# One core, eight batches of attention and a two-layer block: a written order that runs to the end of batch 2 and holds the loads, batch 0's exp sums by adds, 128-column products, half-width output tiles

## The chip, the core and the metric

The kernel runs on one core of a Trainium2 chip. The metric is the time of one execution in device microseconds; lower is better. The core has five engines with a queue each: TensorE (PE, with its weight loads as PEld), VectorE (DVE), ScalarE (ACT), GpSimd (POOL) and SyncE (SP). The kernel is written so that each engine works through its own instructions in the order in which the program names them, and waits where another engine or a transfer isn't done.

## The reference

Inputs are q, k and v of shape (8, 12, 448, 64) and two weight matrices, all float32; the output is (3584, 768) in float32.

```python
scores = q @ k^T / sqrt(64)
e = exp(scores - max)
attn = e / (sum(e) + exp(-max) + 1e-9)
x = (attn @ v), heads side by side        # (8*448, 768)
h = x @ w_in                              # (3584, 2048)
out = relu(h)**2 @ w_out                  # (3584, 768)
```

The kernel computes exp of the scores without the maximum, and 1 / (sum + 1) for the divisor, which is the same; constant scales (`GS`, L43) are taken out in the last copy.

## The kernel before

**Tiling.** A batch is 448 tokens. Its 12 heads are taken in three quads of four heads; the 448 keys of a head in seven chunks of 64. Scores of one chunk and one quad are four products on quarters of the array (64 rows by 64 columns, shape 64*64 in the profile), which run side by side and write one `sp` tile of two banks; one exp on ScalarE turns it into float16. Such a pair is a visit. Sums of exps for later batches come from adds on VectorE (`add_quad`, L384, four steps) and one product with ones for the quad (`sums_of_quad`, L400); then Ln and Exp on ScalarE give the reciprocal (`quad_z`, L412), products with v give the values (`values_step`, L424, seven steps), and VectorE multiplies both into `xt` (`quad_x`, L436). First-layer blocks are 128 of the 2048 hidden columns: six products of 128 rows each, relu (`relu`, L469, on either engine) into `rt`, and a square on VectorE (`squared`, L476) into `gs`. An output half-tile is 128 tokens by 384 columns: 16 products over the hidden blocks (`out_piece`, L553), then a scaled copy (`out_done`, L569) and a store (`store`, L539, in SP's queue).

**Shapes of the products.** `product` (L457) issues one product of 128*128, or, in mode COLS2, two of 128*64. Mode SQUARE, for output tiles among scores (L744), splits each into four products of 64*64. Transposes (L202, L228) are of shape 128*64.

**Batch 0** is done in two halves of 224 queries, so that its first-layer blocks can start early. One piece is `half_scores` (L262), `half_exp` (L283) and `post` (L298), which multiplies the exps with v and with ones for the sum. The sums of a half are so on TensorE: a product for every key chunk. `half_z` (L318) and `half_x` (L324) follow. `xp`, the tile of values and sums, has one buffer.

**The written order.** From the start to the middle of batch 2 the program is a list of steps, `ORDER` (L684): s scores, e exp, p post, z and x the end of a half, T and U a transpose and its copy, a S Z v X the steps of a quad, i r g a first-layer block of a half of batch 0 (a pair of blocks of 224 columns), q R G a pair of blocks of batch 0 by row tiles (`Square`, L505: 64*64 products, with a no-op of SP's queue between the two halves of the contraction), o O an output half-tile, W warm-up products, c t u the first quad's casts, transposes and copies, P the change from two product tiles (beside `xp`) to a ring of four (L678). Products in the list are in mode COLS2 (L682). Steps s0 to s23 and e0 to e23 are batch 0, s24 and later the quads of batches 1 and 2, seven visits each. The list ends with s55, that is four visits into the second quad of batch 2, and after three output half-tiles (`EARLY`, L44).

**Loads** are GpSimd's (DMA with a cast to float16), issued in this order: batch 0's other quads, v of batch 0, w_in in quarters (each in two issues), batch 1's q and k and v, then with step L0 batch 2's first two quads and w_out in quarters, with L1 the rest of batch 2 and the copy of batch 3 into a float16 stage in DRAM. Natural q and k lie in two tiles, `nn0` and `nn1`, one buffer each, so a load into one waits for the transposes that read it.

**Behind the list** runs a loop over b (L770). For b = 2 it does the 16 first-layer blocks of batch 1 in mode COLS2, visits of batch 2 between output half-tiles in mode SQUARE, and values of batch 2's first two quads. From b = 3 on each pass is the same: values and visits among output half-tiles, then eight blocks, visits among output tiles, and eight more blocks; q and k come transposed by DMA in SP's queue (L168), with a copy on GpSimd (L179) and a stage for the batch after the next. The end is products alone, in mode FULL.

Of the kernel before, what the change touches and what calls it, by code (L numbers as in the profile page):

```python
# [16 lines left out]
def kernel(  # L17
# [26 lines left out]
    EARLY = 3  # L44
    IN_HALVES = 8
# [13 lines left out]
    osb_pool = ctx.enter_context(tc.tile_pool(name="osb", bufs=2))  # L59
# [32 lines left out]


    def mm(out_, lhsT, rhs, start, stop):
        return nc.tensor.matmul(out_, lhsT, rhs, start=start, stop=stop)  # L95
# [202 lines left out]
    def post(at):  # L298

        g, half, _ = HALVES[at]  # L300
        if (g, half) not in xzs:
            xzs[g, half] = xp_pair()
        xz, e = xzs[g, half], half_e(g, half)
        two = pieces(at)
        todo = sorted(two[0] + two[1])
        for is_sum in range(2):
            for c, j in todo:
                for i in range(2):
                    r = slice(64 * i, 64 * i + 64)
                    key = (g, half, i, j)  # L310
# [3 lines left out]
                    opened.add(key)  # L314
# [140 lines left out]
    ots = {}  # L455
# [49 lines left out]
    class Square:  # L505


        def __init__(self, t0, f0):
            self.t0, self.f0 = t0, f0
            self.hp, self.done, self.last = None, 0, None  # L510

        def part(self, flip, c0, c1):
            if self.hp is None:
                self.hp = [mp_tile(), mp_tile()]
            hp, xt = self.hp, xts[self.t0 // S]
            assert flip == self.done // DCH
            for dc in range(c0, c1):
                self.done += 1
                for o in range(2):
                    r = (o + flip) % 2  # L520
                    rows_ = slice(64 * r, 64 * r + 64)
                    for y in (0, 64):
                        f = (self.f0 + o) * 128 + y
                        got = mm(hp[o][y:y + 64, 0:S], win[rows_, dc, f:f + 64], xt[rows_, dc, :],
                                 start=self.done == 1, stop=self.done == 2 * DCH)
                        if self.last:
                            after(got, self.last)
                            self.last = None
            if self.done == DCH:
                self.last = nc.sync.nop()  # L530
                after(self.last, got)

        def relu(self, o, act):
            relu(self.hp[o], (self.t0, self.f0 + o), S, act)

        def squared(self, o):
            squared((self.t0, self.f0 + o), self.t0, S, self.f0 + o, 1)

    def store(c, ot, n0, n1):  # L539
        end = c + 128  # L540
        while c < end:
# [6 lines left out]
            nc.sync.dma_start(out=rows[t, p:p + m, :], in_=ot[o:o + m, n0:n1])  # L548
# [65 lines left out]
    nat0 = nat.tile([128, RUN * 2 * S], FP16, name="nn0")  # L614
    load_natural_quads(0, (1, 2), 0, nat0)
    for g in range(NQ):
        load_v_quads(0, g, g + 1)
    NW = 4
    for i in range(NW):
        load_win(i, NW)  # L620
    load_natural_quads(1, (0,), 0, nat.tile([128, RUN * 2 * S], FP16, name="nn1"))
    load_v_quads(1)
    load_natural_quads(1, (1, 2), 0, nat.tile([128, RUN * 2 * S], FP16, name="nn0"))
# [9 lines left out]
    squares = [Square(0, f0) for f0 in range(IN_HALVES, NFFB, 2)]  # L633

    def loads_later():
        load_natural_quads(2, (0, 1), 0, nat.tile([128, RUN * 2 * S], FP16, name="nn1"))
        for n0 in (0, HALF):
            for y in range(2):
                load_wout(n0, y, 2)

    def loads_last():
        load_natural_quads(2, (2,), 0, nat.tile([128, RUN * 2 * S], FP16, name="nn0"))
        load_v_quads(2)
        stage(3)

    def quad_visit(n):
# [17 lines left out]
        "q": lambda n, flip, c0=0, c1=DCH: squares[n].part(flip, c0, c1),  # L664
        "R": lambda n, o, act: squares[n].relu(o, act),
        "G": lambda n, o: squares[n].squared(o),
# [15 lines left out]
    mode[0] = COLS2  # L682

    ORDER = """  # L684
        W9 c0,0,0 c1,0,0 t0,0,0 c1,4,1 c0,4,0 t1,0,0 u0,0,0,0 u1,0,0,0 t1,0,4 t0,0,4 u1,0,4,1 s0 u0,0,4,0 t1,1,0
        u1,1,0,0 t0,1,0 s1 u0,1,0,0 t0,1,4 e0 t1,1,4 u0,1,4,0 e1 u1,1,4,0 s2 T0,1,1 T0,1,0 U0,1,1 s3 T0,2,0 e2
        e3 U0,1,0 s4 T0,2,1 s5 e4 U0,2,0 p0 s6 p1 e5 e6 s7 e7 p2 p3 U0,2,1 s8 z0 s9 e8 x0 e9 p4 s10 p5 s11 e10
        p6 p7 s12 e11 z1 e12 s13 x1 p8 s14 e13 p9 e14 s15 e15 p10 p11 s16 s17 z2 x2 e16 p12 s18 p13 e17 e18 s19
        p14 s20 p15 e19 z3 i0,3 i0,0 x3 r0,3,0 e20 p16 s21 r0,0,1 p17 s22 p18 T1,0,0 g0,3 e21 g0,0 e22 U1,0,0
        p19 s23 T1,0,1 i0,1 U1,0,1 z4 s24 x4 e23 s25 e24 p20 p21 s26 e25 e26 p22 r0,1,0 s27 p23 z5 T1,1,0 g0,1  # L690
        U1,1,0 i0,2 x5 s28 T1,1,1 r0,2,1 i1,1 e28 U1,1,1 L0 g0,2 e27 i1,0 r1,1,1 s29 r1,0,1 g1,1 s30 T1,2,1 a0,0
        g1,0 U1,2,1 e29 i1,2 s31 e30 a0,1 a0,2 r1,2,1 s32 g1,2 P0 T2,1,0 e32 e31 a0,3 i1,3 T1,2,0 L1 s33 U2,1,0
        r1,3,1 U1,2,0 q1,0,0,3 e33 s34 v0,0 g1,3 q1,0,3,6 e34 S0 v0,1 q1,1,0,3 v0,2 s35 v0,3 a1,0 q1,1,3,6 v0,4
        v0,5 R1,0,0 Z0 s36 e35 R1,1,1 v0,6 G1,0 e36 s37 X0 T2,1,1 T2,0,0 e37 s38 T2,0,1 e38 U2,1,1 s39 q0,0,0,3
        G1,1 s40 q0,0,3,6 e39 s41 U2,0,1 e40 U2,0,0 v1,0 q0,1,0,3 s42 a1,1 a1,2 e41 v1,1 a1,3 q0,1,3,6 v1,2 S1
        R0,1,0 e42 v1,3 a2,0 R0,0,1 s43 v1,4 q2,0,0,3 Z1 v1,5 q2,0,3,6 v1,6 X1 s44 e43 G0,1 G0,0 q2,1,0,3 e44
        s45 q2,1,3,6 e45 R2,0,0 q3,0,0,3 R2,1,1 s46 q3,0,3,6 s47 e46 e47 v2,0 q3,1,0,3 s48 v2,1 G2,1 G2,0
        q3,1,3,6 v2,2 e48 s49 a2,1 v2,3 R3,0,0 e49 R3,1,0 s50 G3,1 o1,0,4 a2,2 s51 G3,0 a2,3 v2,4 e50 o1,4,8
        v2,5 e51 s52 a3,0 S2 v2,6 e52 o2,0,4 o1,8,12 o2,4,8 a3,1 o1,12,16 Z2 X2 s53 e53 s54 o2,8,12 o0,0,4 a3,2
        e54 a3,3 T2,2,0 O1 U2,2,0 S3 s55 o0,4,8 T2,2,1 o0,8,12 o2,12,16 U2,2,1 O2 e55 o0,12,16 Z3 O0  # L700
# [28 lines left out]
    del outs[0:EARLY]  # L729

# [39 lines left out]
    for b in range(2, B):  # L770
        m = NQ * (b - 1)
        if b > 2:
            n = min(3, len(outs))
            ns = 12 * PIECE + n * TILE + KC * PIECE
            work = chain(timed(values_quad(m - 1)), second(n))
# [62 lines left out]
```

## Time and profile before

| what | value |
|---|---|
| time, median of 3 runs | 407.54 us (407.45 to 409.01) |
| the profiled execution: its time | 407.19 us |
| the profiled execution: its span, first to last instruction | 405.4 us |
| granted TensorE clock | 1.000 |
| time to landing of a quarter of w_out (768 KB) | 15.6 us |
| DMA, whole span | 45.38 MB, mean 112 GB/s |

Sizes of the loads as the profile lists them: q or k of one quad 224 KB, v of one quad 224 KB, an issue of w_in 384 KB, one of w_out 768 KB, the stage of q or k 676 KB, v of a whole batch 672 KB, and for batch 0's first quad q and k in two parts, 224 KB each in float32 and 112 KB each in float16.

How to read it: a row of the timeline has the start in us, the time, the engine, the line, the operation, out<-in, shapes and the count of merged instructions, and in brackets the idle time before it with what ended it. `64*64`, `128*64` and `128*128` are rows by columns of the array that a product uses. Products overlap in the records (their ends are modelled), so rates are taken from start to start. A row of groups has, behind the bar, the busy time, the mean ns of one instruction and the idle time before it. A row of DMA issues has the count, the KB of each and the median us to landing.

### The profile page before, as it was taken

The numbers are of one execution on the slowest core, as the hardware profiler recorded it, in microseconds if no ns is written. First come the engines' busy times: TensorE is split into PE (matmuls) and PEld (weight loads), VectorE is DVE, ScalarE is ACT, GpSimd is POOL, SyncE is SP. The second block draws the span as 40 slices with busy tenths as digits, with TensorE's granted clock in tenths as the row PEclk, the third lists the DMA queues.
The fourth block names the chain that finished last, engine by engine and source line by source line (L and its number), as shares of the span: only waits on it lengthen the run. The fifth ranks groups of instructions, "written<-read, shape, count | busy, mean of one in ns | idle before, by whom it ended". The sixth has DMA issues, their size and how long they took to land.

```text
span 405.4 us, 14903 instructions
## 1 busy us (share of the span) xinstructions
PE 392.2 (97%) x6861; PEld 260.8 (64%) x6861; DVE 258.9 (64%) x466; ACT 222.0 (55%) x279; POOL 60.1 (15%) x95
## 2 busy tenths in 40 slices
PE   8878999999999999999999999999999999999996
PEld 4656856657676766767676666767566675555654
DVE  3214778776967777686867777686867868186000
ACT  4897899718375565827475564827366473100111
POOL 8444220005000320006000430005000000000000
PEclk9999999999999999999999999999999999999999
DMA  8999999196908693196907593196401020100222
GB/s 147 204 205 204 204 204 212 31 191 123 213 9 128 140 183 85 42 189 112 222 12 150 118 185 83 42 189 104 103 3 40 3 81 2 57 23 0 79 78 78
DMA packets 70846, 45.38 MB, mean 112 GB/s; under 512 B 46720, under 2 KB 65280, under 8 KB 70784
## 3 DMA queue, kind: packets, MB, share of 16 engines
q0 software_dynamic: 24720, 22.62, 35.6%
q1 hardware_dynamic: 45776, 21.59, 23.5%
q8 instruction: 53, 0.87, 0.9%
q10 hardware_dynamic: 288, 0.23, 0.2%
q14 instruction: 9, 0.07, 0.1%
HBM read 45.69 MB, written 17.93 MB: 157 GB/s over the span
## 4 chain that ended last, share of the span: by engine, by line
PE 86%; DMA 6%; ACT 2%; DVE 2%; POOL 2%; issue 1%; POOLq 0%; DVEq 0%
PE mp L95 76%; PE sp L95 9%; DMA nn<-in_k_dram 3%; DMA win<-in_moe_w_in_dram 3%; PE mp L206 1%; ACT et L245 1%; POOL nn L124 1%; POOL vn L112 1%; ACT rt L472 0%; DVE gs L478 0%; DVE rt L474 0%; DVE xt L441 0%; DVE half L392 0%; DVE half L390 0%; ACT rcp L416 0%
## 5 line engine op out<-in xcount | busy, mean ns | idle before, releaser
L95 PE MATMUL mp<-wout,gs 64*64 64x384 f16 (+3 forms) x2784 | 164.3, 322 | 0.7 <-issue 0.7
L95 PE MATMUL mp<-xt,win 128*64 128x448 f16 (+3 forms) x1632 | 154.1, 342 | 0.7 <-issue 0.7
L95 PEld LDWEIGHTS <-win 128*64 128x64 f16 (+2 forms) x1632 | 90.1, 109 | 57.6 <-issue 4.9
L245 ACT ACTIVATE et<-sp 128x896 f16<-128x896 f32 (+1 forms) x131 | 112.9, 889 | 23.9 <-PE sp L95 20.3
L95 PEld LDWEIGHTS <-gs 64*64 64x64 f16 (+2 forms) x2784 | 100.1, 106 | 39.6 <-issue 3.2
L474 DVE TENSOR_SCALAR rt<-mp 128x448 f16<-128x448 f32 x95 | 59.1, 623 | 19.3 <-PE mp L95 16.0
L472 ACT ACTIVATE rt<-mp 128x448 f16<-128x448 f32 x33 | 18.0, 545 | 78.7 <-PE mp L95 66.9
L95 PE MATMUL sp<-qk 64*64 64x224 f16 (+1 forms) x1056 | 58.4, 274 | 0.6 <-ACT et L245 0.3
L478 DVE TENSOR_TENSOR gs<-rt 128x448 f16<-128x448 f16 x128 | 50.0, 392 | 13.0 <-ACT rt L472 9.2
L245 ACT ACTIVATE nn<-sp 128x896 f16<-128x896 f32 x42 | 37.6, 913 | 14.0 <-PE sp L95 13.4
L95 PEld LDWEIGHTS <-qk 64*64 64x64 f16 x1056 | 34.0, 115 | 16.8 <-issue 7.6
L187 POOL COPY flatq<-qk 64x384 f16<-64x384 f16 x20 | 14.1, 725 | 193.0 <-DMA qk<-stage_k 192.7
L577 DVE TENSOR_SCALAR ot<-mp 128x384 f32<-128x384 f32 x38 | 21.1, 554 | 26.6 <-PE mp L95 26.3
L581 ACT ACTIVATE ot<-mp 128x384 f32<-128x384 f32 (+2 forms) x16 | 7.5, 472 | 50.9 <-PE mp L95 50.9
L95 PEld LDWEIGHTS <-vn 64*64 64x64 f16 x756 | 23.2, 107 | 13.9 <-issue 6.5
L441 DVE TENSOR_TENSOR xt<-mp,rcp 128x448 f16<-128x448 f32 x42 | 24.2, 619 | 10.5 <-PE mp L95 8.6
L95 PE MATMUL mp<-et,vn 64*64 64x448 f16 x420 | 26.8, 349 | 0.2 <-issue 0.2
L415 ACT ACTIVATE rcp<-sp,one_b 128x896 f32<-128x896 f32 x21 | 21.1, 1004 | 6.3 <-PE sp L95 6.3
L578 DVE SCALAR_TENSOR_TENSOR ot<-mp,ot 128x384 f32<-128x384 f32 x38 | 21.2, 558 | 4.0
L390 DVE TENSOR_TENSOR half<-et 128x1792 f16<-128x1792 f16 x15 | 16.3, 1088 | 7.8 <-ACT et L245 7.8
L416 ACT ACTIVATE rcp<-rcp 128x896 f32<-128x896 f32 x21 | 20.0, 951 | 0.7
L392 DVE TENSOR_TENSOR half<-half,et 128x1792 f16<-128x1792 f16 x15 | 16.7, 1110 | 0.1
(57 smaller groups left out, 198.3 us busy)
## 6 DMA issues: line engine op xcount, KB each, us to landing
out_dram<-ot SPq DMA_DIRECT2D x27, 192.0 KB, 3.1
out_dram<-ot SPq DMA_DIRECT2D x9, 384.0 KB, 2.5
win<-in_moe_w_in_dram POOLq DMA_DIRECT2D x8, 384.0 KB, 13.0
wout<-in_moe_w_out_dram POOLq DMA_DIRECT2D x4, 768.0 KB, 15.6
vn<-in_v_dram POOLq DMA_DIRECT2D x10, 288.0 KB, 6.2
stage_q<-in_q_dram POOLq DMA_DIRECT2D x4, 676.0 KB, 9.7
stage_k<-in_k_dram POOLq DMA_DIRECT2D x4, 676.0 KB, 13.6
nn<-in_q_dram POOLq DMA_DIRECT2D x8, 224.0 KB, 10.3
```

Source lines behind the costliest of these rows:

```text
L95: return nc.tensor.matmul(out_, lhsT, rhs, start=start, stop=stop)
L245: nc.scalar.activation(out=out_, in_=in_, func=AF.Exp, scale=scale)
L390: nc.vector.tensor_add(esq[m], a[:, 0:w], a[:, w:2 * w])
L392: nc.vector.tensor_add(esq[m], esq[m], z[:, 0:w])
L415: nc.scalar.activation(out=rcp, in_=zp[:, :, 0:S], func=AF.Ln, bias=one_b)
L416: nc.scalar.activation(out=rcp, in_=rcp, func=AF.Exp, scale=-1.0)
L441: nc.vector.tensor_mul(xts[b][:, 2 * g + i, :], xqs[m][i][:, 0:S], zqs[m][:, i, :])
L472: nc.scalar.activation(out=rt[:, 0:m], in_=hp[:, 0:m], func=AF.Relu)
L474: nc.vector.tensor_scalar(out=rt[:, 0:m], in0=hp[:, 0:m], scalar1=0.0, scalar2=None, op0=ALU.max)
L478: nc.vector.tensor_mul(gs[:, f0:f0 + per, t0 % RING:t0 % RING + n], r, r)
L577: nc.vector.tensor_scalar(out=ot[:, n0:n0 + w], in0=op[:, 0:w], scalar1=OUT_SCALE, scalar2=None, op0=ALU.mult)
L578: nc.vector.scalar_tensor_tensor(out=ot[:, n0:n0 + w], in0=lo[:, 0:w], scalar=OUT_SCALE, in1=ot[:, n0:n0 + w], op0=ALU.mult, op1=ALU.add)
```

## The change

`ORDER` is rewritten and goes on to the end of batch 2's scores (s65), with batch 1's first-layer blocks (j, k, l: `later_in`, relu, square) and six output half-tiles in it (`EARLY` = 6). Batch 0's blocks are all half blocks (i); the row-tiled `Square` and its no-op are gone. The loop begins at b = 3. The line that set mode COLS2 ahead of the list is gone, so products in it are 128*128. Step d issues a load (`LOADS`): 0 to 7 are the quads of q and k, batch by batch without the first, 8 to 13 v of batches 0 and 1 by quads, 14 v of batch 2, 15 to 18 w_in's quarters, 19 to 22 w_out's, 23 the stage of batch 3, 24 batch 3's transposed loads, tail keys, v and the stage of batch 4. `post` keeps only the products with v; b adds the exps of a half on VectorE in four steps and y makes one product for each quarter of the array. O names the engine of the scaled copy. Output tiles are of half width, four buffers, and each is stored when it is done.

```diff
-    EARLY = 3
-    IN_HALVES = 8
+    EARLY = 6
...
-    osb_pool = ctx.enter_context(tc.tile_pool(name="osb", bufs=2))
+    osb_pool = ctx.enter_context(tc.tile_pool(name="osb", bufs=4))
...
-        todo = sorted(two[0] + two[1])
-        for is_sum in range(2):
-            for c, j in todo:
...
-                    mm(xz[64 * j:64 * j + 64, i, is_sum * FIRST:(is_sum + 1) * FIRST],
-                       ones[r] if is_sum else vns[0][r, j, g, c, :], e[r, j, c], start=key not in opened,
-                       stop=bool(is_sum) and c == KC - 1)
+        for c, j in sorted(two[0] + two[1]):
...
+                mm(xz[64 * j:64 * j + 64, i, 0:FIRST], vns[0][r, j, g, c, :], e[r, j, c],
+                   start=key not in opened, stop=False)
...
+    def half_add(g, half, step):
+        e = half_e(g, half)
+        if step == 0:
+            ess[g, half] = es_pool.tile([128, 4 * S], FP16, name="half")
+        t = ess[g, half][:, 0:4 * FIRST].rearrange("p (j c n) -> p j c n", j=2, c=2)
+        if step == 0:
+            nc.vector.tensor_add(t, e[:, :, 0:2], e[:, :, 2:4])
+        elif step == 1:
+            nc.vector.tensor_add(t, t, e[:, :, 4:6])
+        elif step == 2:
+            nc.vector.tensor_add(t[:, :, 0], t[:, :, 0], t[:, :, 1])
+        else:
+            nc.vector.tensor_add(t[:, :, 0], t[:, :, 0], e[:, :, 6])
+    def half_sum(g, half):
+        xz = xzs[g, half]
...
+                mm(xz[64 * j:64 * j + 64, i, FIRST:2 * FIRST], ones[r], t[r, j, 0], start=False, stop=True)
...
+    def later_in(f0, c0, c1):
+        if c0 == 0:
+            hps["later", f0] = mp_tile()
+        hp, xt = hps["later", f0], xts[1]
+        for dc in range(c0, c1):
+            product(hp[:, 0:S], win[:, dc, f0 * 128:(f0 + 1) * 128], xt[:, dc, :], start=(dc == 0), stop=(dc == DCH - 1))
...
-        last = tok + 128 == NT
-        if last:
-            store(tok, ot, n0, n0 + w)
-        elif not first and (n0 == 0 or n0 + w == DM):
-            store(tok, ot, 0, DM)
+        store(tok, ot, n0, n0 + w)
...
+    def load_quad(b, g):
+        x = {(0, 1): (0, 0), (0, 2): (0, 1), (1, 0): (1, 0), (1, 1): (0, 0), (1, 2): (0, 1),
+             (2, 0): (1, 0), (2, 1): (1, 1), (2, 2): (0, 0)}[b, g]
+        if (b, x[0]) not in nats:
+            nats[b, x[0]] = nat.tile([128, RUN * 2 * S], FP16, name=f"nn{x[0]}")
+        load_natural_quads(b, (g,), x[1], nats[b, x[0]])
...
+    LOADS = ([lambda b=b, g=g: load_quad(b, g) for b in range(3) for g in range(NQ) if b + g]
+             + [lambda b=b, g=g: load_v_quads(b, g, g + 1) for b in range(2) for g in range(NQ)]
+             + [lambda: load_v_quads(2)]
+             + [lambda i=i: load_win(i, NW) for i in range(NW)]
+             + [lambda n0=n0, y=y: load_wout(n0, y, 2) for n0 in (0, HALF) for y in range(2)]
+             + [lambda: stage(3), load_third])
...
-    mode[0] = COLS2
...
+        W6 d0 d1 d8 c0,0,1 c1,0,1 t0,0,0 c0,4,1 c1,4,0 u0,0,0,0 t1,0,0 t1,0,4 u1,0,0,0 t0,0,4 u1,0,4,0 s0 t0,1,0
+        u0,0,4,0 t1,1,0 u0,1,0,0 u1,1,0,0 s1 t0,1,4 d2 e0 e1 s2 t1,1,4 u0,1,4,0 e2 T0,1,0 u1,1,4,0 U0,1,0 s3 e3
+        T0,1,1 U0,1,1 s4 s5 e4 e5 T0,2,0 b0,0 d9 T0,2,1 b0,1 s6 b0,2 p0 e6 U0,2,1 s7 e7 p1 U0,2,0 s8 b1,0 d3 p2
+        s9 e8 e9 p3 s10 b0,3 b1,1 s11 e10 y0 T1,0,1 b1,2 T1,0,0 z0 e11 s12 e12 U1,0,0 x0 U1,0,1 b1,3 d4 d10 s13
+        p4 s14 d18 e13 p5 p6 d17 e14 d15 b2,0 p7 y1 z1 T1,2,0 s15 e15 s16 e16 d5 T1,1,0 b2,1 d16 b2,2 x1 b2,3
+        b3,0 s17 b3,1 p8 s18 d11 p9 p10 p11 e17 U1,2,0 s19 y2 b4,0 U1,1,0 e18 z2 s20 x2 b3,2 b3,3 T1,2,1 e19
+        T1,1,1 U1,2,1 s21 e20 p12 p13 p14 s22 p15 y3 e21 s23 e22 b5,0 e23 i0,6 z3 U1,1,1 s24 d6 b4,1 d13 s25
+        b5,1 i0,4 e24 b4,2 e25 x3 b5,2 d22 r0,6,0 r0,4,0 s26 p16 d7 p17 p18 p19 b4,3 e26 g0,6 s27 d21 i0,7 y4
+        g0,4 d12 r0,7,0 e27 z4 s28 s29 e28 i0,5 i0,0 s30 a0,0 x4 e29 g0,7 b5,3 p20 e30 r0,5,0 p21 p22 d19 p23
+        s31 r0,0,0 y5 s32 g0,5 T2,0,0 g0,0 d20 a0,1 e31 i0,1 s33 e32 z5 U2,0,0 s34 e33 r0,1,0 T2,0,1 x5 U2,0,1
+        a0,2 e34 i0,2 r0,2,1 s35 s36 g0,1 g0,2 e35 P0 i1,5 T2,1,0 s37 v0,0 e36 a0,3 S0 r1,5,1 g1,5 i1,4 v0,1
+        a1,0 v0,2 e37 v0,3 v0,4 v0,5 v0,6 U2,1,0 Z0 d23 X0 s38 s39 r1,4,1 e38 i0,3 i1,2 s40 e39 s41 e40 i1,1
+        a1,1 r0,3,0 T2,1,1 g0,3 e41 s42 g1,4 a1,2 r1,1,0 r1,2,1 g1,1 g1,2 a1,3 s43 i1,3 e42 e43 a2,0 U2,1,1
+        T2,2,1 a2,1 i1,0 U2,2,1 a2,2 s44 r1,3,1 v1,0 v1,1 d14 v1,2 v1,3 e44 r1,0,0 v1,4 v1,5 v1,6 s45 S1 o1,0,4
+        a2,3 o1,4,8 i1,7 o1,8,12 e45 Z1 s46 S2 X1 e46 o1,12,16 g1,3 Z2 r1,7,0 O1,0 i1,6 s47 v2,0 v2,1 v2,2 v2,3
+        v2,4 v2,5 e47 v2,6 s48 g1,0 X2 s49 j0,0,2 r1,6,1 j0,2,4 e48 T2,2,0 j0,4,6 g1,7 e49 s50 s51 j13,0,2 g1,6
+        U2,2,0 j11,0,2 k0,1 e50 j11,2,4 e51 o0,0,4 s52 s53 j13,2,4 e52 j13,4,6 j11,4,6 o0,4,8 l0 s54 a3,0 e53
+        s55 e55 o0,8,12 a3,1 j10,0,2 e54 k13,0 k11,0 a4,0 j9,0,2 o0,12,16 s56 a3,2 s57 j10,2,4 O0,0 j10,4,6 l13
+        e56 k10,1 o3,0,4 j1,0,2 e57 l10 j1,2,4 a3,3 j1,4,6 l11 s58 s59 e59 e58 o3,4,8 j9,2,4 j9,4,6 o3,8,12 d24
+        o3,12,16 k9,0 s60 O3,0 s61 j4,0,2 l9 j14,0,2 k1,1 e60 a4,1 j3,0,2 j4,2,4 j4,4,6 j14,2,4 o5,0,4 e61
+        o5,4,8 j3,2,4 k4,0 j15,0,2 j14,4,6 j15,2,4 S3 l4 Z3 a4,2 a4,3 s62 j3,4,6 l1 o5,8,12 k14,0 k3,0 j6,0,2
+        j6,2,4 j2,0,2 j2,2,4 j15,4,6 o5,12,16 j2,4,6 j6,4,6 l14 e62 s63 l3 k15,0 O5,1 v3,0 a5,0 k2,1 v3,1 l15
+        v3,2 v3,3 v3,4 s64 v3,5 k6,0 v3,6 l2 e63 s65 j12,0,2 j12,2,4 j12,4,6 k12,1 X3 j7,0,2 j7,2,4 j8,0,2 l12
+        j8,2,4 j5,0,2 e64 e65 o4,0,4 a5,1 o4,4,8 a5,2 j7,4,6 l6 o4,8,12 j8,4,6 j5,2,4 k8,1 j5,4,6 k7,0 o4,12,16
+        a5,3 v4,0 l8 v4,1 S4 v4,2 v4,3 S5 k5,1 v4,4 v4,5 Z4 v4,6 o2,0,4 l5 o2,4,8 O4,1 o2,8,12 X4 o2,12,16 Z5 l7
+        O2,0
...
     complete(S)
     del outs[0:EARLY]
+    complete(2 * S)
...
-    for b in range(2, B):
+    for b in range(3, B):
```

More of the change, by code (lines that the diff above doesn't have):

```diff
@@ L503, in half_in @@
                         start=(dc == 0 and jf == 0), stop=(dc == DCH - 1 and jf == 1))
[L505 to L537, printed above, removed]
     def store(c, ot, n0, n1):
@@ L613 @@
     load_first_second()
[L614 to L617, printed above, removed]
     NW = 4
[L619 to L623, printed above, removed]
     def keep_warm(n):
@@ L632, with load_third @@
     N0 = len(HALVES)
[L633 to L644, printed above, removed]
+    nats = {}
+    def load_quad(b, g):
[4 more added lines that the diff above has]
+        load_natural_quads(b, (g,), x[1], nats[b, x[0]])
+    def load_third():
+        transposed_loads(3)
+        tail_keys(3)
+        load_v_quads(3)
+        stage(4)
+    LOADS = ([lambda b=b, g=g: load_quad(b, g) for b in range(3) for g in range(NQ) if b + g]
[4 more added lines that the diff above has]
+             + [lambda: stage(3), load_third])
     def quad_visit(n):
@@ L663 @@
         "g": lambda half, pair: squared((half, pair), half * FIRST, FIRST, 2 * pair, 2),
-        "q": lambda n, flip, c0=0, c1=DCH: squares[n].part(flip, c0, c1),
-        "R": lambda n, o, act: squares[n].relu(o, act),
-        "G": lambda n, o: squares[n].squared(o),
+        "b": lambda n, step: half_add(n % NQ, n // NQ, step),
+        "y": lambda n: half_sum(n % NQ, n // NQ),
+        "j": lambda f0, c0=0, c1=DCH: later_in(f0, c0, c1),
+        "k": lambda f0, act: relu(hps.pop(("later", f0)), ("later", f0), S, act),
+        "l": lambda f0: squared(("later", f0), S, S, f0, 1),
+        "d": lambda n: LOADS[n](),
         "a": lambda m, step: add_quad(m, step),
@@ L768 @@
     TILE = NFFB * STEP
-    for b in range(2, B):
+    for b in range(3, B):
         m = NQ * (b - 1)
[L772 to L775, printed above, removed]
-            between([(m, c) for c in range(KC)] + [(m + 1, c) for c in range(4)], work, ns, {10: [m]})
+        n = min(3, len(outs))
+        ns = 12 * PIECE + n * TILE + KC * PIECE
+        work = chain(timed(values_quad(m - 1)), second(n))
+        between([(m, c) for c in range(KC)] + [(m + 1, c) for c in range(4)], work, ns, {10: [m]})
         mode[0] = COLS2
```

54 lines of the change are left out of this document (17 added, 37 removed).

## The prediction

> **What bounds the kernel now.** I read the page first, then the busy time by stretches of ten microseconds, then TensorE's timeline, and from that the stage the change rewrites.
>
> ```profile
> span 405.4 us, 14903 instructions
> PE 392.2 (97%) x6861; PEld 260.8 (64%) x6861; DVE 258.9 (64%) x466; ACT 222.0 (55%) x279; POOL 60.1 (15%) x95
> ...
> 10.00:20.00 10.00, 8.12 (x236) 6.78 (x231) 3.03 (x5) 8.30 (x13) 4.65 (x7) 1.00 1.25 204
> 20.00:30.00 10.00, 6.93 (x210) 5.68 (x204) 1.50 (x3) 9.66 (x16) 3.83 (x6) 1.00 1.24 205
> 30.00:40.00 10.00, 8.95 (x239) 6.87 (x236) 4.83 (x10) 7.66 (x12) 4.60 (x7) 1.00 1.26 204
> 50.00:60.00 10.00, 9.75 (x207) 5.91 (x199) 7.39 (x13) 9.75 (x12) 3.38 (x5) 1.00 1.32 205
> 60.00:70.00 10.00, 9.82 (x199) 6.72 (x195) 7.85 (x15) 9.66 (x13) 0.00 (x0) 1.00 1.20 211
> 100.00:110.00 10.00, 9.68 (x135) 6.20 (x129) 8.90 (x16) 4.70 (x7) 0.82 (x2) 1.00 1.20 208
> ```
>
> In the rows of stretches the columns are PE, PEld, DVE, ACT, POOL, granted clock, DMA share, GB/s. TensorE sets the end, but not alone: from 20 to 30 us it is busy for 6.93 while ScalarE has 9.66, so there the exps are the pace; DMA runs full at about 204 GB/s until 70 us. The clock is 1.00 throughout and drops out.
>
> ```profile
> 6.88 0.57 PE L95 MATMUL sp<-qk 64*64 64x224 f16 x8
> 36.32 0.57 PE L95 MATMUL sp<-qk 64*64 64x448 f16 x8
> 80.59 9.25 PE L95 MATMUL mp<-xt,win 128*64 128x448 f16 x96
> ...
> 108.44 4.54 PE mp L95 x48
> 154.29 4.54 PE mp L95 x48
> 200.14 4.54 PE mp L95 x48
> ...
> 352.72 18.32 PE L95 MATMUL mp<-xt,win 128*128 128x448 f16 x96
> 370.88 31.40 PE L95 MATMUL mp<-wout,gs 128*128 128x384 f16 x208
> ```
>
> These are rows of TensorE's timeline and, in the middle, of the chain of waits. The first score visit s0 starts at 6.88. The first scores 448 wide, s24 (with s25), start at 36.32. The written order ends at 80.59, and the loop pass b = 2, whose last block of products starts at 108.44, ends at 108.44 + 4.54 = 112.98. From there on the same block comes back every 45.85 us (154.29 - 108.44, 200.14 - 154.29). That part keeps its work, so the change is worth what happens to **the 112.98 us**.
>
> The last two rows give a price. 96 products of 448 columns start at 352.72 and the next kind at 370.88: 18.16 / 96 = 0.189 us each. I call that a **slot**. A score visit, a values step or a quad's sum is one slot (four quarter-array products side by side), a transpose step T two, a first-layer block (i or j) six, an output half-tile 16 x 384 / 448 = 13.7.
>
> Behind s24, up to 112.98, the kernel before has 367 slots: 42 visits, 35 values steps, 7 for sums, 7 for posts, 20 for ten transposes, 30 for five i blocks, 48 for the row-tiled blocks, 96 for batch 1's blocks, 82 for six half-tiles. That is 367 x 0.189 = 69.5 us of the 76.7 us (112.98 - 36.32) used. So 7.2 us go elsewhere, and part of it can be priced:
>
> ```profile
> 68.77 0.39 PE L95 MATMUL sp<-qk 64*64 64x448 f16 x4
> 69.11 0.84 PE L95 MATMUL mp<-wout,gs 128*64 128x384 f16 x8
> 69.88 0.38 PE L95 MATMUL sp<-qk 64*64 64x448 f16 x4
> 70.10 0.36 PE L95 MATMUL mp<-et,vn 64*64 64x448 f16 x4
> 70.39 0.84 PE L95 MATMUL mp<-wout,gs 128*64 128x384 f16 x8
> ...
> 343.46 1.52 PE L95 MATMUL mp<-nn,vn 64*64 64x448 f16 x28
> 344.91 0.34 PE L95 MATMUL mp<-wout,gs 128*128 128x384 f16 x1
> ```
>
> **A change of tile shape costs.** The visit at 68.77 should give way after one slot, at 68.96; the 128*64 products start at 69.11, 0.15 late. Eight of these take 4 x 0.162 = 0.65 us, yet the quarter-array products come at 69.88, 0.12 late; at 70.39 the loss is 0.10. From 64*64 to 128*128, 28 products (7 slots, 1.32) begin at 343.46 and the next shape at 344.91: 0.13. I take 0.12 a change. About 24 lie between s24 and 112.98, so 2.9 us; the other 4.3 are stalls.
>
> The Trainium skill speaks against this change here: "TensorEngine Tiling (Array Packing)", section "Key Properties", says that changing the tiling mode, and not just the tile, drains TensorE. The trace agrees, with 0.10 to 0.15 us each time; the page gives no price, so the sum stays as it is.
>
> **The change part by part.**
>
> *Early stage, up to s24.* Sums of batch 0 leave TensorE:
>
> ```profile
> L95 PE MATMUL xp<-et,ones 64*64 64x224 f16 x168 | 8.9, 256 | 0.0
> L394 DVE TENSOR_TENSOR half<-half 128x896 f16<-128x896 f16 x21 | 13.4, 636 | 0.7
> L478 DVE TENSOR_TENSOR gs<-rt 128x448 f16<-128x448 f16 x128 | 50.0, 392 | 13.0 <-ACT rt L472 9.2
> L474 DVE TENSOR_SCALAR rt<-mp 128x448 f16<-128x448 f32 x95 | 59.1, 623 | 19.3 <-PE mp L95 16.0
> ```
>
> 168 products, half as wide and four at a time, are 21 slots (4.0 us); six new sums of four products are 3 slots (0.6). Two thirds of the gain (posts p0 to p15) falls ahead of s24, where ScalarE is the pace, and is worth nothing there. VectorE gets 24 adds, two of 896 and two of 448 a half: 6 x (2 x 0.636 + 2 x 0.392) = 12.3 us. 18 of them are written ahead of s24, in stretches where VectorE is busy 1.50 to 4.83 of 10, so I cost them at nothing; without that cover a late add delays y, then z, x and the next p.
>
> What s24 waits for is the exp two visits earlier, e22:
>
> ```profile
> 1.19 4.02 PE L95 MATMUL xp<-warm 128*128 128x512 f16 x9 [1.19 <-DVE warm L600]
> 5.14 0.64 PE L232 MATMUL mp<-ident,flatq 128*64 128x128 f16 x4
> ...
> 17.23 2.98 ACT L245 ACTIVATE et<-sp 128x896 f16<-128x896 f32 x4
> 20.09 0.64 ACT L321 ACTIVATE rcp<-xp,one_b 128x448 f32<-128x448 f32 x1
> 28.48 0.64 ACT L321 ACTIVATE rcp<-xp,one_b 128x448 f32<-128x448 f32 x1 [0.25 <-PE xp L95]
> 29.63 0.90 ACT L245 ACTIVATE et<-sp 128x896 f16<-128x896 f32 x1
> 36.75 2.54 ACT L245 ACTIVATE et<-sp 128x896 f16<-128x896 f32 x3 [1.51 <-PE sp L95]
> ...
> 20.55 13.17 DMA nn<-in_k_dram
> 33.76 0.30 PE L206 MATMUL mp<-ident,nn 128*64 128x128 f16 x3 [0.15 <-DMA nn<-in_k_dram]
> 34.74 0.49 PE L206 MATMUL mp<-ident,nn 128*64 128x128 f16 x11 [0.69 <-issue]
> ```
>
> Three full exps and a half one take 20.09 - 17.23 = 2.86 us, a full one about 0.81, and a z 29.63 - 28.48 = 1.15. Exp e20, with z0 to z3 done, ends at 29.63 + 0.90 = 30.53. Before, s24 came 5.8 us later, because TensorE had transposes of batch 1 ahead of it, and the keys of that quad landed only at 20.55 + 13.17 = 33.72, behind all of w_in; ScalarE stood 1.51 us. After, these keys are loaded ahead of w_in, their transposes are written into the exp-paced part, and only one block (i0,6) stands before s24. I drop z3 from ScalarE's time (30.53 - 1.15), add e21 and e22 (1.62), and take 0.6 off for three warm-up products fewer (the nine start at 1.19 and take 4.02, and the transposes behind them start at 5.14; the first visit that needs a load is still held by it): e22 ends at 30.4. On TensorE s23 may start at 29.6, i0,6 takes 6 slots and two changes (1.4), so **s24 starts at 31.2**. Bounds: 30.0 if nothing stalls, 36.3 if nothing is gained.
>
> *Loads.* They are moved within POOL's queue; the bytes stay.
>
> ```profile
> win<-in_moe_w_in_dram POOLq DMA_DIRECT2D x8, 384.0 KB, 13.0
> ...
> 35.54 0.70 POOL L124 DMA_DIRECT2D nn<-in_q_dram  x1 [5.02 <-PE mp L206]
> ```
>
> At 204 GB/s the sizes add up so: ahead of w_in's last quarter, the first to be used, go 3.7 MB, with it 4.4 MB, landed at 2.5 + 4.4 / 0.204 = 24 us; i0,6 comes at 30. The last half of w_out closes 12.0 MB, at 61 us; o0, which needs it, is written 39 us behind s24, at 70. The first issue of a load with a wait (batch 1's second quad, whose buffer batch 0's transposes must free, about 12.5 us as before) has 2.5 MB queued ahead, enough until 15 us; w_in and v behind it on POOL lose nothing. The third batch's transposes wait in SP's queue behind two stores, some 27 us before their use. Price of the edit: nothing. Were the wait 5 us longer, w_in would come at 29 us, still in time.
>
> *From s24 to the end of the stage.* The new order has 42 visits, 35 values steps, 6 sums and 1 for two half sums, 7 for eight posts, 12 for six transposes, 90 for fifteen i blocks, 96 for j blocks, 82 for half-tiles: 371 slots, 70.2 us. With products of 128 columns every step from scores to products is a change of shape, where the row-tiled blocks had none: I count 51 changes behind s24 (41 between 64*64 and 128*128), 51 x 0.12 = 6.1 us, 3.2 more than before. Bounds for the 128*128 kind, of which one row speaks: 0.08 and 0.22 (the 0.12 and a load of 128 columns not hidden):
>
> ```profile
> L95 PEld LDWEIGHTS <-gs 128*128 128x128 f16 x256 | 24.4, 98 | 15.1 <-issue 0.4
> ```
>
> *Stalls there.* Before they were 4.3 us, with ScalarE at 9.75 and 9.66 of 10 from 50 to 70 us. After, 42 exps at 0.81 are 34 us, three half z's at 1.15 and six quad z's of at most twice that 17, nine relus or copies at no more than 0.62 some 5: 56 us in 76, so ScalarE is no longer the pace. VectorE takes over for a while: between s24 and i0,2 the ring has two buffers, and each block waits for the relu of the one two before it. 22 VectorE instructions are written there: six relus at 0.623, eight adds' worth of batch 0 and quad 0 with two x's, a copy and squares, 12.6 us by their rows, about 11.5 with the overlap of neighbours, against 11.3 on TensorE. Equal loads that feed each other don't run free: I take 1.5 us there and 0.9 for the rest, where the ring has four and VectorE is written far ahead: 2.4. Bounds 0 and 5.4.
>
> *Output half-tiles.* Four halves in place of two whole tiles; each is stored when done. No wait for a store shows among the waits, and the last token block was stored in pieces already. 18 more issues on SP, under the products: nothing; exposed, it would cost the last stores' time alone.
>
> **The sum:** 31.2 + 70.2 + 6.1 + 2.4 = 109.9 against 112.98: 3.1 us less. The profiled execution took 407.19 us with its span of 405.4; the median of the runs is 407.54, 0.35 above it. 407.54 - 3.1 = **404.5**.
>
> **The rivals.**
> 1. *The 128-column weights aren't loaded across a change of shape.* At each of the 41 changes between 64*64 and 128*128 the first load lies bare, 0.22 in place of 0.12, and 4.1 us are added: the stage ends at 114.0 and the time is 408.6. At 0.25 each it is 409.8, slower. It decides from 0.12 + 3.1 / 41 = 0.20 on. Against it: the one row of that kind shows 0.13, load included.
> 2. *VectorE paces the stage, slower.* Adds, relus and x's go through one queue. If each of the six half sums comes 0.4 us late, s24 slips by 2.3; if the two-buffer part, with 11.5 us of VectorE's work, runs no fuller than 8 of 10, as most of its stretches, it takes 14.4 in place of the 12.8 forecast, and the adds for the quads behind it slip by as much again: 3.1 more. In all 5.4: the stage ends at 115.3, 409.9. It takes the gain from 3.1 on and is slower from 5.2. For it: equal loads. Against: VectorE is 64% busy over the span, and reaches 8.90 of 10 in one stretch.
> 3. *No change:* s24 gains half (33.7), the rest as forecast: 112.4, 407.0.
> 4. *The loads don't do what is written:* POOL stands at a buffer, DMA idles, s24 is no earlier (36.3): 115.0, 409.6. For it: before, POOL did stand 5.02 us for a transpose. Against: DMA's share stayed at 1.2 all the same.
>
> **Chances.** What a measurement tells from no change is 0.5%, 2.04 us: faster lies below 405.5, slower above 409.6. Forecast 0.52, its own range 400.5 to 405.5. Rival 1: 0.15, two thirds of it slower. Rival 2: 0.13, slower. Rival 3: 0.12, no change. Rival 4: 0.08, slower. So faster 0.52, same 0.17, slower 0.31. The low end, 400.5, is s24 at 30.0, no stalls and 0.11 a change (105.8, 7.2 less); the high end, 411.0, lies past rivals 1, 2 and 4 by a little.
>
> **What would show it.** TensorE's timeline: s24 (the first 448-wide scores) near 31, then the first 4.54 us block of four 128*64 first-layer tiles with the steady period behind it ending near 110. Gaps of 0.12 at 64*64 to 128*128; gaps of 0.2 or more mean rival 1. Waits of TensorE for relus between 31 and 45 us above 2 us mean rival 2; waits for loads, or POOL rows with waits over 3 us before 15 us, rival 4. The steady period must stay 45.85; if it moves, the half-tiles matter and the sum is wrong there.

## The result

The changed kernel takes **404.81 us** (4 runs, 404.44 to 405.19) against 407.69 (4 runs) of the kernel before: a ratio of 0.9923, 95% interval 0.9899 to 0.9947. On a second chip 12 runs of it gave 406.0 (401.09 to 407.64) against 407.16, ratio 0.9940 (0.9912 to 0.9969). The ratios here and below compare fast runs: two of these 12, and one of e4's six, count as slow and are left out of them, but not of the medians. It is faster; the forecast was 404.5. The sum behind it was not as good as its end.

From the page and the timeline of the changed kernel (TensorE, then the chain of waits, as in the prediction):

```profile
span 402.7 us, 13781 instructions
PE 393.0 (98%) x6234; PEld 255.6 (63%) x6234; DVE 264.8 (66%) x484; ACT 222.3 (55%) x282; POOL 61.5 (15%) x97
...
33.45 0.57 PE L92 MATMUL sp<-qk 64*64 64x448 f16 x8
111.79 0.40 PE L92 MATMUL sp<-qk 64*64 64x224 f16 x8
...
153.17 4.54 PE mp L92 x48
199.01 4.54 PE mp L92 x48
```

And of the kernel before, the first scores of batch 3 and a piece of its chain:

```profile
112.91 0.40 PE L95 MATMUL sp<-qk 64*64 64x224 f16 x8
...
246.22 4.54 PE mp L95 x48
286.86 0.73 issue
293.14 4.54 PE mp L95 x48
```

Batch 3's first scores (64x224) close the stage that was rewritten. So the span splits in three:

| | before | changed | forecast |
|---|---|---|---|
| to s24 | 36.32 | 33.45 | 31.2 |
| s24 to batch 3's first scores | 76.6 | 78.3 | 78.7 |
| from there to the end of the span | 292.5 | 290.9 | 292.5 |

The stage gained 1.1 us, not 3.1. The later passes, where the work is the same, are 1.6 us shorter, though the period stands at 45.84 (199.01 - 153.17). In the profile of before TensorE stands there once for nothing that the profile names ("issue", 0.73 at 286.86); in the changed kernel's it does not. The pass around that pause takes 46.92 us in the chain of before and one ahead of it 46.08, in place of 45.85, which makes 1.3 of the 1.6 us. The other 0.3 lies at the end of the span, behind the start of the last block of products.

**Why s24 isn't at 31.2.** The early rows of the changed kernel, TensorE first, then POOL, and the stretch from 10 to 20 us (columns as in the prediction):

```profile
12.00 0.96 PE L198 MATMUL mp<-ident,nn 128*64 128x128 f16 x14
14.56 1.71 PE L198 MATMUL mp<-ident,nn 128*64 128x128 f16 x28
16.20 0.58 PE L92 MATMUL sp<-qk 64*64 64x224 f16 x8
34.98 1.31 PE L92 MATMUL mp<-xt,win 128*128 128x224 f16 x12 [0.95 <-DMA win<-in_moe_w_in_dram]
...
16.58 0.70 POOL L116 DMA_DIRECT2D nn<-in_q_dram  x1 [8.21 <-PE mp L198]
...
10.00:20.00 10.00, 8.46 (x147) 6.52 (x146) 6.08 (x12) 6.55 (x10) 3.42 (x5) 1.00 0.89 135
```

28 transposes take 14.56 to 16.20, 1.64 us; before, 28 of the same began at 9.75 and the next kind at 10.65, 0.9. Fourteen have 0.96 for 0.58. TensorE runs at about half its rate up to 16.2 us, though the column of the granted clock says 1.00. ScalarE, then the pace, is busy 6.55 of 10 where it was 8.30. POOL waits 8.21 us for these transposes at the first load with a wait, and DMA falls from 204 to 135 GB/s; w_in then comes late for the second block (0.95), which it doesn't where POOL stands 5.14 us (e1, below).

### The profile page after: what moved, and what is told of

Read it like the earlier page. It is cut to its first block, busy times and chain, and to the rows that moved or that the text cites. A ratio compares the mean times of both kernels' runs of the same rounds, so it can differ in the third digit from the quotient of the medians.

```text
span 402.7 us, 13781 instructions
## 1 busy us (share of the span) xinstructions
PE 393.0 (98%) x6234; PEld 255.6 (63%) x6234; DVE 264.8 (66%) x484; ACT 222.3 (55%) x282; POOL 61.5 (15%) x97
## 4 chain that ended last, share of the span: by engine, by line
PE 91%; DMA 4%; POOL 1%; ACT 1%; DVE 1%; issue 0%; ACTq 0%
PE mp L92 79%; PE sp L92 10%; DMA win<-in_moe_w_in_dram 3%; PE mp L198 2%; ACT et L237 1%; PE mp L224 1%; DMA et<-in_q_dram 1%; POOL nn L116 1%; POOL win L134 0%; DVE half L404 0%; PE xp L92 0%; POOL vn L104 0%; ACT rt L485 0%; DVE qk L203 0%; DVE half L408 0%
## 5 line engine op out<-in xcount | busy, mean ns | idle before, releaser
L92 PE MATMUL mp<-wout,gs 64*64 64x384 f16 (+2 forms) x2592 | 164.3, 322 | 0.0
L92 PE MATMUL mp<-xt,win 128*64 128x448 f16 (+2 forms) x1344 | 153.5, 340 | 1.1 <-DMA win<-in_moe_w_in_dram 1.0
L92 PEld LDWEIGHTS <-win 128*64 128x64 f16 (+1 forms) x1344 | 89.2, 106 | 60.5 <-issue 8.8
L92 PEld LDWEIGHTS <-gs 64*64 64x64 f16 (+1 forms) x2592 | 98.2, 106 | 40.7 <-issue 2.0
L92 PEld LDWEIGHTS <-qk 64*64 64x64 f16 x1056 | 32.9, 117 | 22.9 <-issue 13.4
L564 ACT ACTIVATE ot<-mp 128x384 f32<-128x384 f32 (+2 forms) x18 | 8.5, 473 | 52.0 <-PE mp L92 52.0
L560 DVE TENSOR_SCALAR ot<-mp 128x384 f32<-128x384 f32 x35 | 19.4, 554 | 23.6 <-PE mp L92 23.4
L92 PEld LDWEIGHTS <-vn 64*64 64x64 f16 x756 | 21.6, 107 | 8.4 <-issue 0.9
L92 PE MATMUL mp<-et,vn 64*64 64x448 f16 x420 | 23.2, 349 | 0.0
L561 DVE SCALAR_TENSOR_TENSOR ot<-mp,ot 128x384 f32<-128x384 f32 x35 | 19.5, 558 | 3.7
```

The lines of the kernel that those rows point to most:

```text
L560: nc.vector.tensor_scalar(out=ot, in0=op[:, 0:w], scalar1=OUT_SCALE, scalar2=None, op0=ALU.mult)
L561: nc.vector.scalar_tensor_tensor(out=ot, in0=lo[:, 0:w], scalar=OUT_SCALE, in1=ot, op0=ALU.mult, op1=ALU.add)
```

## The experiments

Theory: three warm-up products fewer leave TensorE slow, and this holds back exps and loads. Rivals: the loads alone; the adds; the shape of the products; the output tiles. Each edit is to the changed kernel, b4 to the one before. The runs are from three chips, on which the kernel before has medians of 406.94 to 407.16. The last three columns are of one profiled execution, and the last is the span behind batch 3's first scores. That execution is the fastest of its kernel's runs in e4 and e9 and the slowest in e2, e6 and e8.

| run | time, us (runs) | ratio to before, 95% interval | s24 | s24 to batch 3 | rest |
|---|---|---|---|---|---|
| e1 nine warm-up products | 403.56 (6) | 0.9902 (0.9870 to 0.9934) | 31.14 | 77.5 | 292.7 |
| e2 128*64 products | 405.05 (12) | 0.9961 (0.9934 to 0.9988) | 34.75 | 78.6 | 293.0 |
| e3 sums on TensorE | 403.56 (11) | 0.9931 (0.9901 to 0.9961) | 31.66 | 78.8 | 290.9 |
| e4 whole output tiles | 402.5 (6) | 0.9888 (0.9850 to 0.9925) | 29.77 | 78.1 | 291.7 |
| a1 unaltered | 406.0 (12) | 0.9940 (0.9912 to 0.9969) | 36.17 | 77.5 | 291.4 |
| e6 twelve | 403.54 (6) | 0.9904 (0.9876 to 0.9932) | 33.17 | 77.5 | 293.7 |
| e5 nine, w_in earlier | 410.09 (7) | 1.0054 (1.0035 to 1.0073) | 37.86 | 77.3 | 292.7 |
| b4 keys earlier | 407.39 (12) | 1.0004 (0.9985 to 1.0023) | 35.80 | 76.2 | 293.2 |
| e7 nine, free slot | 402.06 (6) | 0.9877 (0.9844 to 0.9910) | 30.51 | 77.4 | 291.1 |
| e8 nine, 128*64 | 405.6 (12) | 0.9955 (0.9934 to 0.9976) | 30.83 | 79.6 | 295.9 |
| e9 nine, sums on TensorE | 403.22 (6) | 0.9901 (0.9875 to 0.9928) | 30.71 | 78.8 | 290.8 |
| e10 nine, whole tiles | 402.59 (6) | 0.9894 (0.9864 to 0.9923) | 29.90 | 77.9 | 292.9 |

**e1 and a1: the warm-up.**

```diff
-        W6 d0 d1 d8 c0,0,1 ...
+        W9 d0 d1 d8 c0,0,1 ...
```

> The changed kernel with nine warm-up products in place of six. Theory (TensorE runs slowly until 16 us because the warm-up was cut, and this holds back the exps): transposes and first scores at half their time, s24 at 31.3 us instead of 33.45, the time 402.8, 2.0 us less than the changed kernel's 404.8. Rival (the early loss is POOL standing 8.2 us at a buffer and the loads behind it): s24 stays within 0.5 us of 33.45 and the time within 0.5 us of 404.8.

> The changed kernel unaltered, on the chip of these runs. Theory (six warm-up products leave it to chance whether TensorE is at full speed from 5 us or only from 16 us, and s24 moves by 3.7 us with it): times in two groups, about 401.5 to 403 and 404.5 to 406; median near 404. Rival (the spread of the kernels with six products came from their own edits): all within 0.5 us of 404.8.

Nine products, TensorE and POOL:

```profile
10.43 0.58 PE L198 MATMUL mp<-ident,nn 128*64 128x128 f16 x14
12.23 0.97 PE L198 MATMUL mp<-ident,nn 128*64 128x128 f16 x28
31.14 0.57 PE L92 MATMUL sp<-qk 64*64 64x448 f16 x8
...
13.52 0.70 POOL L116 DMA_DIRECT2D nn<-in_q_dram  x1 [5.14 <-PE mp L198]
```

The transposes are at full rate, POOL stands 3 us less, and s24 comes at 31.14, as expected. The time is 403.56, 0.8 above what was expected, and its interval overlaps those of the unaltered kernel; that nine are faster in time is likely, not shown by this run alone. Six products, unaltered (a1):

```profile
11.93 0.96 PE L198 MATMUL mp<-ident,nn 128*64 128x128 f16 x14
25.16 0.58 PE L198 MATMUL mp<-ident,nn 128*64 128x128 f16 x14 [1.06 <-DMA nn<-in_q_dram]
28.33 0.59 PE L92 MATMUL xp<-et,vn 64*64 64x224 f16 x8 [1.33 <-DMA vn<-in_v_dram]
30.90 1.99 PE L198 MATMUL mp<-ident,nn 128*64 128x128 f16 x28
36.17 0.57 PE L92 MATMUL sp<-qk 64*64 64x448 f16 x8
```

Slow again, and here the loads behind POOL's wait hold a transpose for 1.06 and a post for 1.33 us. Behind these waits TensorE is at half its rate a second time: from 28 to 34 us the granted clock is 0.50, and 28 transposes take 1.99 us (1.18 in the changed kernel's first profile, where the clock stays at 1.00). So s24 comes at 36.17, 2.7 us later than there, though the two are alike to within 0.1 us up to 24 us. The whole-tile kernel e4, whose start is the same six products, drew the other lot:

```profile
9.74 0.58 PE L198 MATMUL mp<-ident,nn 128*64 128x128 f16 x14
29.77 0.57 PE L92 MATMUL sp<-qk 64*64 64x448 f16 x8
```

Nothing that differs between e4 and a1 lies ahead of s24, and it moves by 6.4 us. So chance decides; the theory had this right, but not the amount: three of a1's 12 runs lie below 404, nine from 405.6 to 407.6, and its median is 406.0, not 404. Which start each of these runs had is not on record, only that of the profiled one. In the five profiles with six products s24 lies between 29.77 and 36.17, in the five with nine and no load moved back (e1, e7 to e10) between 29.90 and 31.14. e1's six runs lie between 401.2 and 405.3.

**e6: twelve.** The same edit with W12.

> The changed kernel with twelve warm-up products. Theory: full speed from the first transposes in every run, which start 1.3 us later than with nine; s24 at 32.4, the time 404.0 with a spread under 2 us but for stalls of the instruction stream. Rival (more warm-up is always better): below the 403.6 of nine.

In the profile s24 came 2.0 us later than with nine (33.17; 0.8 more than expected): TensorE waits 1.41 us for the third part of v, and behind that the granted clock is 0.50 from 28 to 30 us. So full speed in every run does not hold. This profile is of the slowest of the six runs (406.16); the median is the same as with nine, 403.54. More than nine brings nothing in time.

**e5, e7 and b4: the loads.**

```diff
 e5, with W9
-        ... d9 T0,2,1 ... s14 d18 e13 p5 p6 d17 e14
+        ... d9 d18 d17 T0,2,1 ... s14 e13 p5 p6 e14
 e7, with W9
-             (1, 1): (0, 0), (1, 2): (0, 1),
+             (1, 1): (0, 0), (1, 2): (1, 1),
-        ... b1,0 d3 p2 ... b1,3 d4 d10 s13
+        ... b1,0 d4 p2 ... b1,3 d10 d3 s13
 b4: load_natural_quads(1, (0,), ...) moved ahead of the loop over load_win
```

> Nine warm-up products, and w_in's last two quarters loaded ahead of batch 1's second quad, so that POOL has work for the queue while it stands for the transposes. Theory (DMA's gap between 15 and 20 us costs only the wait of the second first-layer block for w_in): s24 unchanged at 31.1, no wait for w_in, 402.7, 0.9 less than nine alone. Rival (the keys that now come 3.9 us later hold the transposes of batch 1 and with them the exps): s24 at 33 or later, 405.

> Nine warm-up products, and batch 1's third quad loaded into the free half of the second buffer, ahead of the second quad, so that POOL has no transposes to wait for there; v's last part comes ahead of the load that does wait. Theory (with POOL standing, the loads come late and hold transposes, posts and the second block): POOL's wait shorter than 3 us, no wait of TensorE for a load behind 16 us, s24 at 30.3, the time 402.3, 1.2 less than nine products alone (403.56). Rival (behind the warm-up the exps alone set s24): s24 at 31.1, 403.5.

> The kernel before with one load moved: batch 1's first quad of q and k ahead of w_in. Theory (s24 was late because these keys landed at 33.7 us): s24 at 34.8 instead of 36.3, the time 1 to 1.5 us less than before, 405.7. Rival (s24 is held by what TensorE and ScalarE have to do ahead of it): s24 within 0.4 us, the time within 0.5 us of before, or more, since w_in comes 2.2 us later.

In e5 the rival won by far, with one wait:

```profile
27.86 0.96 PE L198 MATMUL mp<-ident,nn 128*64 128x128 f16 x14 [6.73 <-DMA nn<-in_q_dram]
```

TensorE stands 6.73 us for batch 1's third quad, now behind half of w_in, and the 14 transposes after it are slow again (0.96; the granted clock is 0.50 from 24 to 32 us). e7 does the opposite. Its third quad goes into the half of the second buffer that lies free:

```profile
13.63 0.71 POOL L116 DMA_DIRECT2D nn<-in_q_dram  x1 [1.28 <-PE mp L198]
27.05 0.71 POOL L116 DMA_DIRECT2D nn<-in_q_dram  x1 [5.17 <-PE mp L198]
...
30.51 0.57 PE L92 MATMUL sp<-qk 64*64 64x448 f16 x8
107.86 0.40 PE L92 MATMUL sp<-qk 64*64 64x224 f16 x8
```

POOL's first wait for transposes is 1.28 us; the long one (5.17) now comes at 27.05, ahead of loads that have slack: behind 14 us TensorE waits for no load longer than 0.2 us up to batch 3's first scores. And 402.06 is the lowest median of all, 0.9877 (0.9844 to 0.9910) of before. s24 and time are as the theory said; against nine alone the intervals overlap. b4 went to its rival: the keys came earlier and nothing moved (s24 0.5 us, the time not at all).

```profile
34.22 0.49 PE L206 MATMUL mp<-ident,nn 128*64 128x128 f16 x11 [0.73 <-issue]
35.80 0.57 PE L95 MATMUL sp<-qk 64*64 64x448 f16 x8
```

The same transposes start at 34.22 where they started at 34.74, and no longer wait for DMA. From 28 us to s24 TensorE has no gap of 0.2 us or more in b4 but the 0.73. In the kernel before, then, it was the work written ahead of s24 that held it.

**e2 and e8: the shape of the products.**

```diff
+    mode[0] = COLS2
     for step in ORDER.split():
```

> The changed kernel with its products in the written order as two of 128*64 again. Theory (a change of shape costs 0.12 us for either shape, and 224-column blocks run 0.09 us slower each as two of 128*64): sixteen blocks, 1.4 us more, 406.2. Rival (the changes between 64*64 and 128*128 are dearer than those to 128*64, by 0.1 us or more each): 4 us less, 401.

> Nine warm-up products, and the written order's products as two of 128*64. Theory (a change of shape costs the same for both; the blocks of 224 columns run 0.09 us slower each): from s24 to batch 3's first scores 78.9 us against 77.5, the time 405.0. Rival (128*128 dearer at a change of shape): under 77 us, 402.5 or less. No difference above 0.4 us: neither.

With six products, start and chance cover the answer. With nine the time is 405.6, 2.0 above e1, as expected, but not for the reason given. Of e8, and of the changed kernel, two pairs of blocks of 224 columns between scores:

```profile
38.10 2.30 PE L92 MATMUL mp<-xt,win 128*64 128x224 f16 x43 [1.55 <-issue]
52.52 2.49 PE L92 MATMUL mp<-xt,win 128*64 128x224 f16 x48
54.94 0.57 PE L92 MATMUL sp<-qk 64*64 64x448 f16 x8
```

```profile
53.45 2.47 PE L92 MATMUL mp<-xt,win 128*128 128x224 f16 x24
55.85 0.57 PE L92 MATMUL sp<-qk 64*64 64x448 f16 x8
```

2.42 us against 2.40: the blocks cost the same in either shape. What e8 has more of is instructions (14555 against 13787 in e1) and waits for none of the other engines ("issue"), 1.55 us in the stage and 2.4 in the later passes, the latter with the granted clock at 0.57 from 242 to 246 us behind it. But this profile is of e8's slowest run (408.28), and e1's has such waits too (0.58 and 1.43). Why the median is 2.0 higher stays open; that fewer instructions make such waits rarer is a guess.

**e3 and e9: the sums.** The products with ones are back in each post, and steps b and y do nothing.

```diff
+        for is_sum in range(2):
...
     for step in ORDER.split():
+        if step[0] in "by":
+            continue
```

> The changed kernel with batch 0's exp sums as products with ones at each post again, and no adds. Theory (the sums' products cost only where TensorE is the pace, behind s24: 6 slots of 0.189 us): 1.1 us more, 405.9. Rival (the 24 adds hold VectorE's other work, and with it TensorE between 31 and 47 us): 1 to 2 us less, 403.

> Nine warm-up products, and batch 0's exp sums on TensorE again, without the adds. Theory (6 slots more behind s24): s24 within 0.5 us of 31.1, 78.6 us behind it against 77.5, the time 404.6. Rival (the adds hold VectorE and TensorE with it): 76.5 us or less behind s24, 402.5.

Behind s24 e9 has 78.8 us against e1's 77.5, as the theory said, and s24 is 0.4 earlier. The times, 403.22 and 403.56, don't tell them apart, nor do e3's. So in the time the adds are worth nothing that these runs could measure; the rival, that they hold TensorE, finds no support either.

**e4 and e10: the output tiles.** Whole tiles, two buffers, stored when both halves are done, as in the kernel before.

> The changed kernel with whole-width output tiles, two buffers, stored when both halves are done. Theory (the halves bring nothing; that the part behind 153 us is 1.3 us shorter than before comes from stalls of TensorE's instruction stream in the profile of before): 404.8 within 0.4. Rival (half tiles shorten the later passes): 406.1.

> Nine warm-up products, and whole-width output tiles. Theory (the halves are worth nothing): 403.6 within 0.5, the period of the later passes 45.85 us. Rival (the whole tiles are better, as the 402.5 with six products might mean): 402.5 or less.

The halves don't shorten the later passes: the part behind batch 3's first scores varies from 290.8 to 293.7 us among kernels with half tiles and products of 128 columns, and is 291.7 and 292.9 with whole ones. The medians of 402.5 and 402.59 are lower than with halves (e1: 403.56), but the intervals overlap (0.9894, 0.9864 to 0.9923, and 0.9902, 0.9870 to 0.9934). Whether whole tiles are 1 us better stays open. One thing does differ a little: from the start of the last 208 products to the end of the span it is 34.2 to 34.4 us in the profiles with half tiles and 34.4 to 35.0 in those with whole ones (before, b4, e4, e10). That is 0.3 us between the changed kernel (34.25) and before (34.52).

## Why the prediction was right, and where it wasn't

Direction, time and range held. By its own steps:

- **s24 at 31.2: wrong for the kernel as it stands, by 2.25 us.** The failed term is "0.6 off for three warm-up products fewer": they cost more than they give. Even where the full rate came early with six, s24 is only 0.13 earlier than with nine (29.77 in e4, 29.90 in e10, which differ in nothing else). With nine, s24 is at 31.14 in e1, a pause of 0.58 in the block ahead of it included, and at 30.51 in e7; the step without its 0.6 gives 31.8. So the rest of it held and was a little too dear.
- **Keys behind w_in as part of what held s24 before: wrong.** b4 moved them and gained nothing, so the order of the loads alone doesn't bring s24 forward (e5 shows that a bad one puts it back). What stands ahead of s24 on TensorE does differ. Before, these were three pairs of blocks of 224 columns, in the changed kernel (last row) one:

```profile
28.36 2.49 PE L95 MATMUL mp<-xt,win 128*64 128x224 f16 x48
35.05 1.34 PE L95 MATMUL mp<-xt,win 128*64 128x224 f16 x24
32.20 1.32 PE L92 MATMUL mp<-xt,win 128*128 128x224 f16 x12
```

No run moved these blocks alone, so their share isn't shown.

- **Loads at nothing: wrong.** The prediction worked out the landing of w_in's last quarter only, and put the end of POOL's wait at 12.5 us. It ended at 16.58, and DMA fell to 135 GB/s: the sign that was named for rival 4, though s24 did come earlier. The second block then waited 0.95 us for w_in, where the prediction had it "still in time". Two more loads stand behind that wait, batch 1's third quad and the third part of v; they held TensorE for 1.06 and 1.33 us in a1 and not at all in the first profile. e5 and e7 show the price of such loads in both directions.
- **371 slots, 51 changes at 0.12, 2.4 of stalls: 78.7 us forecast, 78.3 measured**, 77.3 to 78.8 in the runs with 128-column products (the two highest have 6 slots more). By the prediction's slots and changes 2.0 us are left for stalls, and 0.95 of that is the wait for w_in. The changed kernel's timeline around two visits:

```profile
75.55 0.57 PE L92 MATMUL sp<-qk 64*64 64x448 f16 x8
76.06 1.31 PE L92 MATMUL mp<-xt,win 128*128 128x448 f16 x6
77.20 0.81 PE L92 MATMUL mp<-wout,gs 128*128 128x384 f16 x4
77.94 0.57 PE L92 MATMUL sp<-qk 64*64 64x448 f16 x8
78.45 0.82 PE L92 MATMUL mp<-wout,gs 128*128 128x384 f16 x4
```

Two visits are 2 slots, 0.38: the products come at 76.06, 0.13 late; six slots and four products of 0.162 are due at 77.84 from there, and the scores come at 77.94, 0.10 late. Rival 1 (0.22) is out by these changes and by the sum. Of rival 2 there is no sign: TensorE has no wait for a relu between 31 and 45 us.
- **Later passes unchanged: right as to the work (45.84), but two longer passes in the profile of before, one of them with the pause of 0.73 us, were in the 405.4 that the sum was taken from.** The 1.6 us of that part made up for most of the 2 us missing in the stage. By its stages the kernel did what rival 3 said: s24 at 33.45 (33.7 there), the stage ending at 111.79 (112.4). Rival 3's time was 407.0; that 404.5 came so near is luck in good part. On the second chip the medians differ by 1.2 (ratio 0.9940).
- **Half tiles at nothing: held but for some 0.3 us behind the last products.** The medians show no gain from them.

## What to carry to other kernels

Before cutting a warm-up, look at what the first real instructions cost each: a start that looks earlier by a microsecond can be slow for ten. Where such a start depends on chance, one profile of it says little. Where one queue issues all loads, the price of a wait is what stands behind the waiting load, and each of those needs its slack looked up, not the first user alone. And split a span into stages before believing that a forecast came true: two errors of opposite sign look like none.

## What the runs showed of the hardware

TensorE's rate early in the kernel has two values: 14 transposes of the same shape take 0.58 or 0.96 us. After six warm-up products from 1.19 us on, the full rate came at 4.6 us in one profile (e4), near 5.8 in one (e3) and behind 16.2 in two (the changed kernel and a1). In the fifth, e2, it was there at 5 us, was lost behind a wait of 0.98 us for a load, and came back at 18. With nine it came by 8 us in every profile.

The granted clock shows the half rate in some of these stretches and not in others. Rows from 10 to 20 us, first of the changed kernel, where 14 transposes take 0.96 and the clock reads 1.00, then of e2, where they take 0.96 as well:

```profile
10.00:20.00 10.00, 8.46 (x147) 6.52 (x146) 6.08 (x12) 6.55 (x10) 3.42 (x5) 1.00 0.89 135
10.00:20.00 10.00, 8.74 (x145) 7.00 (x142) 6.08 (x12) 6.40 (x10) 3.77 (x6) 0.59 0.97 152
```

Where the half rate came back later (a1, e5, e6, e8), the clock shows it. So the durations are the safer sign.

The Trainium skill tells of this: by "TensorE: Matmul & The Clock Gate", Part 1, the array runs at half its clock until a stretch of about 3.4 us has been busy, the stretches run free of the kernel's start, so the moment varies, and an idle stretch brings the half rate back. The traces agree with both values, with the chance and with the return (0.96 after the 6.73 us wait in e5). They don't bear out the length: in the changed kernel the half rate lasts beyond 16 us, with TensorE's rows busy for 9.6 of the 10 us from 2 to 12, and in a1 it comes back behind waits of 1.06 and 1.33 us, both shorter. What sets the length here stays open.

Waits of TensorE for nothing that the profile names ("issue") stand in the steady passes of some profiles and not of others. Two of them, of e1 and of e8:

```profile
237.45 0.97 PE L92 MATMUL mp<-wout,gs 64*64 64x384 f16 x17 [1.43 <-issue]
240.84 0.97 PE L92 MATMUL mp<-wout,gs 64*64 64x384 f16 x17 [2.38 <-issue]
```

Their place recurs: in six of the twelve profiles with the new order (e1, e2, e5, e6, e8, e10) such a wait, of 0.44 to 2.38 us, begins 127.4 to 128.0 us behind batch 3's first scores, and both profiles of the old one have 0.73 at the same place (286.86 in before, 286.64 in b4). The size changes from profile to profile; what is waited for isn't shown. Behind batch 3's first scores, where the work is equal, profiles differ by up to 3 us (290.8 to 293.7 in kernels with half tiles and products of 128 columns), as much as the change itself.
